# Attention and ReGLU on one core: V's sums of four in three strips on TensorE, and the plan's durations

## The chip, the cores and the metric

The kernel runs on one core of a Trainium2 chip. The time is that of one execution on the device in microseconds; the kernel before takes 375.14 us, the median of three runs (374.98 to 375.96).

The engines are named as in the profile: PE is TensorE's matmul, PEld its weight load, DVE is VectorE, ACT is ScalarE, POOL is GpSimd, SP the engine that issues most DMAs. SPq and POOLq are the queues of SP and POOL as far as they issue or wait.

## The reference

Two kinds of attention are computed for 8 batches of 8 heads, 576 tokens, 64 numbers a head, and added; the result goes through a feed-forward net.

```python
q_d = q.reshape(B, H, Sd, factor, D).mean(axis=3)     # factor 4, Sd 144; the same for k and v
out_d = sm_attn(q_d, k_d, v_d)                        # softmax attention over 144 pooled tokens
out_up = np.repeat(out_d, factor, axis=2)
mask = np.abs(pos[:, None] - pos[None, :]) < factor   # local attention, 3 tokens to either side
...
attn_out = out_up + out_local
x = attn_out.transpose(0, 2, 1, 3).reshape(B * S, H * D)          # 4608 x 512
gate = np.maximum(x @ w_gate, 0.0)                                # 512 -> 1536
return (gate * (x @ w_val)) @ w_out                               # 1536 -> 512
```

## The kernel before

**Pairs.** `pair(p)` (L392) treats two heads of one batch at once; there are 32 pairs, four to a batch. The first four pairs (`hd`) are the head of the kernel. A pair goes through these steps:

- `lq`, `lk` (L419): SP loads q and k of both heads. `cast` (L332, or L331 on ACT) makes them half precision in `c16`.
- T: q and k are transposed. Pairs 0 to 7 (`p < TD`) do it on TensorE (L439) and copy the result out of PSUM (`ev`); later pairs do it by DMA (L470) into `tq`, and one copy, also called `ev`, interleaves it into `qkT`. That copy may run on ACT, POOL or DVE; its planned durations are the tuple `EV` (L50).
- `pl`: sums of four tokens of q and k (L489 on DVE; in the head by extra matmuls, L443).
- S: local scores (L501, 48 matmuls with 32-column weights) and pooled scores (L520, 12 matmuls with 32-column weights that write four strips of 32 partitions). The local softmax follows on DVE, POOL and ACT (`msk` L558, `mx` L561, `sub` L564, `exp` L567, `sm` L584, `rc` L586, `nrm` L588, and `tr`, a transpose in blocks, L594).
- Pooled softmax: `dmx` (L570), `nb` (L573), `exd` (L578, three activations that write the weights into `wd` and their sums into `smd`), `rcd` (L600, the reciprocals), `nrd` (L603, weights times reciprocals).
- W: the pooled weights are transposed, so that the 144 pooled keys stand in two halves of 72 rows. Pairs 0 to 7 do it on TensorE (L612, six transposes) with a copy out of PSUM (`evw`); later pairs by DMA (L626).
- V: `lv` loads v in windows of 32 tokens that overlap (L646, L652), `vc` casts them into `vw16`. For the first 12 pairs (`p < VPOOL`), VP sums four tokens of V on TensorE (L666): `sums_sb` is a matrix of ones and zeros, 128 x 6 x 72, and for each half of the keys six matmuls accumulate into the same 72 rows, one for each block of windows. `vd` copies the sums into `vdz`. Later pairs load v once more (`l4`, L679) and add on POOL (L683, L688).
- The output: L697 (local, 12 matmuls), L705 (pooled, 4 matmuls with `vdz` as weights and the transposed pooled weights as data), `od` (L715), and `xa` (L721), which writes the pair's rows of `xT`.

**Feed-forward.** `first` (L740) makes one block of the hidden layer: matmuls of `xT` with w_gate and with w_val (L755), the rectifier on ACT (L767), the product on DVE (L775). `second` (L787) makes a block of 128 output tokens (L797, three parts of four matmuls), a copy on ACT (L806) and a store (L809).

**PSUM.** Eight banks: 0 to 3 are pool F (feed-forward, and pairs 1 and 2), 4 to 7 pool A (pairs).

**The plan.** No step is issued where the program text has it. Each is an `Op` with an engine (or several, `add_any`), a duration in us, its dependencies, a priority, the banks it needs, and for a DMA a transfer time `xfer`. `list_schedule` (L82) simulates the engines, one DMA channel, the port that DVE and POOL share, the banks and TensorE's instruction fetch with these durations, and each time issues, on the engine that could start first, the ready step of the lowest priority number. An engine that isn't an op's first choice is charged 0.8 us more in the comparison. The order that comes out is fixed: each engine executes its list in that order, waiting at each instruction for what it needs. So a duration in the plan costs no time itself, but it decides the order on all queues. Weight loads have due times that are constants (`W_AT` L42; `WO_T0`, `WO_DT` L43). The loads of a pair from the second batch on are released by `pacers` (L816): the feed-forward block named there must have been computed first.

Of the kernel before, what the change touches and what calls it, by code (L numbers as in the profile page):

```python
# [46 lines left out]
BIAS = 0.8  # L47
STOP = 0.3

EV = (1.4, 1.4, 1.3)  # L50

# [186 lines left out]
def kernel(  # L238
# [36 lines left out]
    def many(n, shape, dt, name):  # L275
        return [pool.tile(shape, dt, name=f"{name}{i}") for i in range(n)]
# [63 lines left out]
    def half(i):  # L340
# [6 lines left out]
                  name="ld_mask")  # L347
    ld_sums = add(SP, 0.2, lambda o: nc.sync.dma_start(sums_sb, sums_dr), prio=5.8, xfer=0.4,
                  name="ld_sums")
# [29 lines left out]
    for g in range(4):  # L379
        for nm, dst, src in (("g", wg_sb, moe_w_gate), ("v", wv_sb, moe_w_val)):  # L380
            w_ld[nm, g] = add(POOL, 0.95, wpiece(dst, src, 384 * g, 384), prio=-40 + g,
                              xfer=2.55, after=W_AT[g], name=f"w{nm}{g}")
# [9 lines left out]
    def pair(p):  # L392
# [25 lines left out]
        def load(src, odd):  # L418
# [4 lines left out]

        lq = add(SP, 0.1, load(q, 0), [free_nat, pace], prio=PQ, xfer=1.1, name=f"lq{p}")
        lk = add(SP, 0.1, load(k, 1), [free_nat, pace], prio=PQ + 0.5, xfer=1.1,
                 name=f"lk{p}")
        casts = ((POOL, 1.55), (DVE, 1.0), (ACT, 1.5)) if hd else (
            (POOL, 1.19), (DVE, 0.9), (ACT, 1.15))
        n2 = 2 * nj
# [120 lines left out]
        if hd:  # L550
            mxo = add(DVE, 0.55, lambda o: nc.vector.tensor_reduce(
                out=mx[S3], in_=lview(), axis=AX.X, op=ALU.max), [Sx, z_w], prio=P + 23,
                name=f"mx{p}")
            sub = add(DVE, 0.62, lambda o: nc.vector.tensor_tensor(
                out=s_, in0=lview(), in1=bc12(mx[S3]), op=ALU.subtract),
                [mxo, b2.get("exp")], prio=P + 24, free=[("S", p)], name=f"sub{p}")
        else:
# [14 lines left out]
            negate=True), [Sd, b3.get("nrd")], prio=P + 22, name=f"dmx{p}")  # L572
        nb = add(POOL, 0.26, lambda o: nc.gpsimd.tensor_scalar(  # L573
            out=nmb[S3][:, 0:3], in0=nmx[S3][:, 0:3], scalar1=scale / 16.0, scalar2=None,
            op0=ALU.mult), [dmax], prio=P + 22.5, name=f"nb{p}")
# [16 lines left out]
        for par in range(2):  # L592
# [7 lines left out]
        rcd = add(DVE, 0.15, lambda o: nc.vector.reciprocal(  # L600
            out=rsd[S3][:, 0:3], in_=smd[S3][:, 0:3]), exd, prio=P + 27.5, name=f"rcd{p}")
        w3 = [[256, 3], [128, 2], [1, 72]]
        r["nrd"] = nrd = add_any(either(lambda o, e: e.tensor_tensor(  # L603
            out=_sap(wd_, 0, 128, 0, w3), in0=_sap(wd_, 0, 128, 0, w3),
            in1=_sap(rsd[S3], 0, 128, 0, [[1, 3], [0, 2], [0, 72]]), op=ALU.mult),
            (POOL, 0.92), (DVE, 0.62)), [rcd], prio=P + 28.5, name=f"nrd{p}", port=(DVE, POOL))

        def emit_W(o):
            for kc in range(2):
                for i in range(3):  # L610
                    n = 3 * kc + i
                    nc.tensor.transpose(half(o.banks[0])[0:72, 128 * n : 128 * n + 128],  # L612
                                        wd_[:, 2 * i + kc, 0:72], ident)
        if p < TD:
            r["W"] = W = add(PE, 0.34, emit_W, [nrd], prio=P + 30, need=(pool_, 1),
                             key=("W", p), name=f"W{p}", n=6)

            evw = add_any(copies(
                _sap(wT[S3], 0, 72, 0, [[48, 6], [2 * SD, 2], [24, 2], [1, 24]]),
                lambda o: _sap(half(W.banks[0]), 0, 72, 0,  # L620
                               [[128, 6], [64, 2], [32, 2], [1, 24]]),
                (ACT, 0.64), (DVE, 0.74)),
                [W, b3.get("V")], prio=P + 31, free=[("W", p)], name=f"evw{p}")
            wcols = lambda hh, kc: _sap(wT[S3], 0, 72, (2 * hh + kc) * SD, [[1, SD]])
        else:
            r["W"] = evw = add(SP, 1.1, lambda o: nc.sync.dma_start(  # L626
                wT[S3], _sap(wd_, 0, 128, 0, [[1, 768]]), transpose=True),
                [nrd, b3.get("V")], prio=P + 30, xfer=0.8, name=f"dW{p}")
            wcols = lambda hh, kc: _sap(wT[S3], 0, 72, 128 * kc + 64 * hh,
                                        [[256, 3], [32, 2], [1, 24]])  # L630
# [6 lines left out]
        for par in range(2):  # L637
# [18 lines left out]
        r["vcast"] = vc = add_any(copies(  # L656
            vw16[S3], lambda o: vw_, (POOL, 1.5), (DVE, 0.97), (ACT, 1.5)),
            lv + behind + [b3.get("V")], prio=P + 26, name=f"vc{p}", port=(DVE, POOL))

        vdz4 = _sap(vdz[S3], 0, 72, 0, [[320, 2], [128, 2], [1, 64]])  # L660
        if p < VPOOL:

            def emit_VP(o):
                for kc in range(2):
                    for i in range(6):
                        nc.tensor.matmul(  # L666
                            out=bank[o.banks[0]][0:72, 128 * kc : 128 * kc + 128],
                            lhsT=sums_sb[:, i, :], rhs=vw16[S3][:, 6 * kc + i, :],
                            start=(i == 0), stop=(i == 5))
            VP = add(PE, 0.8, emit_VP, [vc, ld_sums], prio=P + 27, need=(pool_, 1),  # L670
                     key=("VP", p), name=f"VP{p}", n=12)
            vps = lambda o: _sap(bank[VP.banks[0]], 0, 72, 0, [[64, 2], [128, 2], [1, 64]])
            vdo = add_any(copies(vdz4, vps, (ACT, 0.39), (DVE, 0.41)), [VP, z_vd[S3], b3.get("V")],
                          prio=P + 27.2, free=[("VP", p)], name=f"vd{p}")
        else:
# [19 lines left out]
        def emit_V(o):  # L695
# [178 lines left out]
```

## Time and profile before

| what | us |
|---|---|
| median of three runs | 375.14 |
| the profiled execution | 373.75 |
| its span | 372.0 |
| TensorE busy | 349.3 |
| POOL busy | 211.7 |
| ACT busy | 193.2 |

The chain of work that ended last lies to 65% on PE, to 14% on DMA and to 8% on POOL. The mean granted TensorE clock was 0.995 of full speed.

A row of a group of instructions reads: line, engine, operation, what it writes and reads, partitions x elements and type, count | busy us, mean ns of one | idle time of the engine just before, and who ended it. A row of the timeline reads: start us, duration us, engine, line, what, count, and in square brackets the engine's idle time before it with what released it. Matmuls overlap in a pipeline, so that their own durations overlap too; what a block of them occupies is read from its first start to the start of the next block.

### The profile page before, as it was taken

How to read it: one execution, taken by the hardware profiler on the slowest of the kernel's cores; microseconds unless marked ns; L12 is line 12 of the kernel's file. 1: busy time of each engine (PE TensorE's matmuls, PEld its weight loads, DVE VectorE, ACT ScalarE, POOL GpSimd, SP SyncE). 2: the span in 40 equal slices, each digit the busy share in tenths (PEclk: the TensorE clock that was granted, in tenths of full speed). 3: DMA queues.
4: the chain of work that ended last, by engine and by line, in shares of the span. 5: the costliest groups of instructions: out<-in, count | busy, mean ns of one | idle time of the engine just before them, and what ended most of it. 6: DMA issues, size and time to landing. Idle time of an engine off the chain costs nothing.

```text
span 372.0 us, 11562 instructions
## 1 busy us (share of the span) xinstructions
PE 349.3 (94%) x4728; PEld 194.2 (52%) x4728; DVE 249.2 (67%) x476; ACT 193.2 (52%) x469; POOL 211.7 (57%) x246
## 2 busy tenths in 40 slices
PE   1869999999999999989999998999999999999995
PEld 1657565646655555435555555445545545455442
DVE  3688867657988977867877986877877782222200
ACT  2595747355677554744745564655655543333311
POOL 6698582854868776578778584846785830000000
PEclk9998999999999999999999999999999999999999
DMA  7989999979999699999999989799899820100022
GB/s 189 196 172 234 239 197 244 170 205 217 207 214 201 191 168 234 188 215 204 215 207 212 202 199 215 201 220 193 198 223 221 124 60 28 58 28 31 28 86 85
DMA packets 125271, 64.31 MB, mean 173 GB/s; under 512 B 101026, under 2 KB 112674, under 8 KB 125218
## 3 DMA queue, kind: packets, MB, share of 16 engines
q1 hardware_dynamic: 119394, 58.85, 75.9%
q0 software_dynamic: 5824, 4.72, 8.7%
q8 instruction: 37, 0.61, 0.7%
q14 instruction: 16, 0.13, 0.1%
HBM read 47.03 MB, written 9.44 MB: 152 GB/s over the span
## 4 chain that ended last, share of the span: by engine, by line
PE 65%; DMA 14%; POOL 8%; SPq 4%; issue 4%; DVE 2%; ACT 2%; POOLq 0%; ACTq 0%
PE bank L755 38%; PE bank L797 18%; DMA vw<-in_v_dram 6%; DMA stage<-in_k_dram 5%; PE bank L501 2%; DMA wT<-wd 2%; POOL e L588 2%; DMA wo_sb<-in_moe_w_out_dram 2%; PE bank L697 2%; SPq L419 2%; POOL vw L332 2%; PE bank L705 2%; POOL c L332 1%; SPq L652 1%; PE bank L666 1%
## 5 line engine op out<-in xcount | busy, mean ns | idle before, releaser
L755 PE MATMUL bank<-xT,wg_sb 128*128 128x512 f16 (+1 forms) x768 | 112.8, 286 | 1.4 <-DVE gT L775 1.2
L755 PE MATMUL bank<-xT,wv_sb 128*128 128x512 f16 (+1 forms) x768 | 112.6, 286 | 0.0
L775 DVE TENSOR_TENSOR gT<-r,bank 128x512 f16<-128x512 f16 (+1 forms) x112 | 74.0, 664 | 51.6 <-PE bank L755 48.7
L797 PE MATMUL bank<-wo_sb,gT 128*128 128x512 f16 x432 | 101.0, 379 | 1.0 <-DMA wo_sb<-in_moe_w_out_dram 0.6
L767 ACT ACTIVATE r<-bank 128x512 f16<-128x512 f32 (+1 forms) x112 | 65.0, 583 | 63.0 <-PE bank L755 58.7
L755 PEld LDWEIGHTS <-wg_sb 128*128 128x128 f16 x768 | 49.2, 98 | 44.8 <-issue 2.2
L755 PEld LDWEIGHTS <-wv_sb 128*128 128x128 f16 x768 | 48.8, 98 | 42.0 <-issue 0.2
L797 PEld LDWEIGHTS <-gT 128*128 128x128 f16 x432 | 40.9, 98 | 47.6 <-issue 1.8
L332 POOL CAST c<-stage 128x1152 f16<-128x1152 f32 (+1 forms) x29 | 34.5, 1189 | 25.1 <-DMA stage<-in_k_dram 25.0
L332 POOL CAST vw<-vw 128x1536 f16<-128x1536 f32 x28 | 41.3, 1476 | 11.8 <-DMA vw<-in_v_dram 9.1
L806 ACT COPY y_sb<-bank 128x512 f32<-128x512 f32 x36 | 21.1, 586 | 50.5 <-PE bank L797 49.7
L578 ACT ACTIVATE wd<-bank,nmb 128x144 f16<-128x144 f32 x96 | 35.6, 382 | 18.9 <-POOL nmb L573 18.8
L594 DVE STREAM_TRANSPOSE at<-e 64x384 f16<-64x384 f16 x64 | 36.5, 570 | 11.7 <-POOL e L588 11.0
L489 DVE TENSOR_REDUCE qkd<-qkT 128x288 f16<-128x1152 f16 x28 | 37.5, 1344 | 4.8 <-ACT qkT L331 4.4
L588 POOL TENSOR_TENSOR e<-e,rs 128x384 f16<-128x384 f16 x32 | 26.6, 832 | 15.1 <-DVE rs L586 10.9
L721 DVE TENSOR_TENSOR xT<-bank,od_sb 128x288 f16<-128x288 f32 x64 | 26.4, 451 | 10.9 <-ACT od_sb L715 9.1
L603 POOL TENSOR_TENSOR wd<-wd,rsd 128x432 f16<-128x432 f16 x32 | 28.9, 906 | 3.2 <-DVE rsd L600 2.9
L683 POOL TENSOR_TENSOR vs<-stage 72x512 f32<-72x512 f32 x20 | 25.3, 1267 | 6.5 <-DMA stage<-in_v_dram 6.4
L331 ACT COPY qkT<-tq 128x1152 f16<-128x1152 f16 x21 | 25.3, 1204 | 5.4 <-DMA tq<-c 5.4
L564 POOL TENSOR_TENSOR s_sb<-s_sb,mx 128x384 f32<-128x384 f32 x27 | 22.5, 834 | 6.1 <-DVE mx L561 4.5
L573 POOL TENSOR_SCALAR nmb<-nmx 128x3 f32<-128x3 f32 x32 | 7.4, 232 | 24.8 <-DVE nmx L570 24.8
L584 DVE TENSOR_REDUCE sm<-e 128x12 f32<-128x384 f16 x32 | 17.6, 549 | 5.1 <-ACT e L567 4.9
(57 smaller groups left out, 329.7 us busy)
## 6 DMA issues: line engine op xcount, KB each, us to landing
vw<-in_v_dram SPq DMA_DIRECT2D x126, 96.0 KB, 4.9
stage<-in_q_dram SPq DMA_DIRECT2D x32, 288.0 KB, 5.0
stage<-in_k_dram SPq DMA_DIRECT2D x32, 288.0 KB, 6.9
out_dram<-y_sb SPq DMA_DIRECT2D x36, 256.0 KB, 2.6
stage<-in_v_dram SPq DMA_DIRECT2D x20, 288.0 KB
wg_sb<-in_moe_w_gate_dram POOLq DMA_DIRECT2D x4, 384.0 KB, 8.4
wv_sb<-in_moe_w_val_dram POOLq DMA_DIRECT2D x4, 384.0 KB, 12.1
wo_sb<-in_moe_w_out_dram POOLq DMA_DIRECT2D x4, 384.0 KB, 6.2
```

Of the source, the lines that this page charges most:

```text
L331: return lambda o: nc.scalar.copy(out=dst, in_=src(o))
L332: return lambda o: engine[eng].tensor_copy(out=dst, in_=src(o))
L489: nc.vector.tensor_reduce(out=qkd[S3].rearrange("p (x t) -> p x t", x=2), in_=qk_sums, axis=AX.X, op=ALU.add)
L578: exd.append(add(ACT, 0.37, lambda o, i=i: nc.scalar.activation(out=wd_[:, 2 * i : 2 * i + 2, 0:72], in_=dview()[:, i, :].rearrange("p (k ...
L588: r["nrm"] = nrm = add_any(either(lambda o, e: e.tensor_tensor(out=e_, in0=e_, in1=bc12(rs[S3]), op=ALU.mult), (POOL, 0.84), (DVE, 0.5)), ...
L594: tr.append(add(DVE, 0.575, lambda o, lo=lo: nc.vector.transpose(out=at2[S3][lo : lo + 64, :, lo // 2 : lo // 2 + 32], in_=e_[lo : lo + 64 ...
L603: r["nrd"] = nrd = add_any(either(lambda o, e: e.tensor_tensor(out=_sap(wd_, 0, 128, 0, w3), in0=_sap(wd_, 0, 128, 0, w3), in1=_sap(rsd[S3 ...
L721: nc.vector.tensor_tensor(out=xT[:, kk, t1 % XR : t1 % XR + 288].rearrange("p (t f) -> p t f", f=4), in0=bank[V.banks[hf]][:, 0:288].rearr ...
L755: nc.tensor.matmul(out=bank[(h or o).banks[0]][:, n * x : n * x + n], lhsT=w_sb[:, kk, bass.ts(jj, 128)], rhs=xT[:, kk, t0 % XR : t0 % XR ...
L767: rl = add(ACT, 0.17 + 0.00083 * n * m, lambda o: nc.scalar.activation(out=rt[:, 0 : n * m], in_=bank[f1.banks[0]][:, 0 : n * m], func=AF. ...
L775: gm = add(DVE, 0.15 + 0.00104 * n * m, lambda o: nc.vector.tensor_tensor(out=gT[:, js[0] : js[0] + m, pos : pos + n], in0=rt[:, 0 : n * m ...
L797: nc.tensor.matmul(out=bank[parts[0].banks[0]], lhsT=gT[:, jj, col : col + 128], rhs=wo_sb[:, jj, :], start=(jj == 0), stop=(jj == NJJ - 1))
```

## The change

VP uses six matmuls of 256 columns instead of twelve of 128. `sums_sb` holds only two patterns of 32 columns (24 of them used, 8 zero); the pooled keys of blocks 2g and 2g + 1, 24 in each half, go to strip g, that is to partitions 32g to 32g + 23, and both halves stand side by side in the 256 columns. For these 12 pairs the keys therefore stand in 96 rows, 24 used and 8 unused in each 32: `exd` writes the weights in runs of 24 with a step of 32, `nrd` multiplies in that shape (so `rcd` writes each reciprocal twice), W transposes 96 columns, `evw` and `vd` copy 96 rows, and L705 contracts over 96 rows. The unused places are zeros, which is why `wd` is zeroed whole at the start. Pairs 12 to 31 keep 72 rows.

Besides, planned durations change: the ev copy (ACT and POOL 1.4 to 1.2, DVE 1.3 to 0.68), S (0.80 to 0.67), VP (0.8 to 0.34, 0.4 in the head), casts, subtractions and POOL's small ops by some hundredths, transfers of q and k (1.1 to 1.0 in the head, to 1.3 after it), of the matrix (0.4 to 0.1), and the issue of gate and value weights (0.95 to 0.85).

```diff
+LQ = (1.0, 1.3)
-EV = (1.4, 1.4, 1.3)
+EV = (1.2, 1.2, 0.68)
...
-    sums = np.zeros((128, 6, 72), np.float16)
-    for i in range(6):
+    sums = np.zeros((128, 2, 32), np.float16)
+    for i in range(2):
...
-    vdz = many(3, [72, 2, 2, 128], FP16, "vdz")
+    vdz = many(3, [96, 2, 2, 128], FP16, "vdz")
-    sums_sb = pool.tile([128, 6, 72], FP16, name="sums_sb")
+    sums_sb = pool.tile([128, 256], FP16, name="sums_sb")
-    rsd = many(3, [128, 4], FP32, "rsd")
+    rsd = many(3, [128, 6], FP32, "rsd")
...
-    z_wd = [zeros(wd[s][:, :, 72:128], (POOL, DVE)[s % 2], -88 + s, 0.2) for s in range(3)]
-    z_vd = [zeros(vdz[s][:], POOL, -90 + s, 0.27) for s in range(3)]
+    z_wd = [zeros(wd[s][:], (POOL, DVE)[s % 2], -88 + s, 0.38) for s in range(3)]
+    z_vd = [zeros(vdz[s][:], POOL, -86 + s, 0.3) for s in range(3)]
...
-            r["S"] = Sx = Sd = add(PE, 0.80, emit_S, [*evs, pl], prio=P + 20, need=(pool_, 2),
+            r["S"] = Sx = Sd = add(PE, 0.67, emit_S, [*evs, pl], prio=P + 20, need=(pool_, 2),
...
+        KR = 96 if p < VPOOL else 72
+        kd_cols = [[128, 2], [32, 3], [1, 24]] if p < VPOOL else [[128, 2], [1, 72]]
+        kd_in = [[72, 2], [24, 3], [1, 24]] if p < VPOOL else [[72, 2], [1, 72]]
...
-                out=wd_[:, 2 * i : 2 * i + 2, 0:72],
-                in_=dview()[:, i, :].rearrange("p (k c) -> p k c", k=2), func=AF.Exp,
+                out=_sap(wd_, 0, 128, 256 * i, kd_cols),
+                in_=_sap(dview()[:, i, :], 0, 128, 0, kd_in), func=AF.Exp,
...
-            out=rsd[S3][:, 0:3], in_=smd[S3][:, 0:3]), exd, prio=P + 27.5, name=f"rcd{p}")
-        w3 = [[256, 3], [128, 2], [1, 72]]
+            out=rsd[S3].rearrange("p (i k) -> p i k", k=2),
+            in_=_sap(smd[S3], 0, 128, 0, [[1, 3], [0, 2]])), exd, prio=P + 27.5, name=f"rcd{p}")
+        w3 = [[128, 6], *kd_cols[1:]]
...
-                    nc.tensor.transpose(half(o.banks[0])[0:72, 128 * n : 128 * n + 128],
-                                        wd_[:, 2 * i + kc, 0:72], ident)
+                    nc.tensor.transpose(half(o.banks[0])[0:KR, 128 * n : 128 * n + 128],
+                                        wd_[:, 2 * i + kc, 0:KR], ident)
...
-                for kc in range(2):
-                    for i in range(6):
+                for x in range(2):
+                    for g in range(3):
                         nc.tensor.matmul(
-                            out=bank[o.banks[0]][0:72, 128 * kc : 128 * kc + 128],
-                            lhsT=sums_sb[:, i, :], rhs=vw16[S3][:, 6 * kc + i, :],
-                            start=(i == 0), stop=(i == 5))
-            VP = add(PE, 0.8, emit_VP, [vc, ld_sums], prio=P + 27, need=(pool_, 1),
-                     key=("VP", p), name=f"VP{p}", n=12)
+                            out=bank[o.banks[0]][32 * g : 32 * g + 32, 0:256],
+                            lhsT=sums_sb[:, 32 * x : 32 * x + 32],
+                            rhs=_sap(vw16[S3], 0, 128, 128 * (2 * g + x),
+                                     [[6 * 128, 2], [1, 128]]),
+                            start=(x == 0), stop=(x == 1))
+            VP = add(PE, 0.4 if hd else 0.34, emit_VP, [vc, ld_sums], prio=P + 27, need=(pool_, 1),
+                     key=("VP", p), name=f"VP{p}", n=6)
...
                     nc.tensor.matmul(
-                        out=bank[o.banks[0]][:, 288 : 288 + SD], lhsT=vdz[S3][:, hh, kc, :],
-                        rhs=wcols(hh, kc), start=(n == 0), stop=(n == 3))
+                        out=bank[o.banks[0]][:, 288 : 288 + SD],
+                        lhsT=vdz[S3][0:KR, hh, kc, :],
+                        rhs=wcols(hh, kc), start=(n == 0), stop=(n == 3))
```

More of the change, by code (lines that the diff above doesn't have):

```diff
@@ L422, in load @@
                 _dap(src, base, [[tk * D, nj], [HS, 2], [1, tk * D]]))
[L424 to L428, printed above, removed]
+        lq = add(SP, 0.1, load(q, 0), [free_nat, pace], prio=PQ, xfer=LQ[hd], name=f"lq{p}")
+        lk = add(SP, 0.1, load(k, 1), [free_nat, pace], prio=PQ + 0.5,
+                 xfer=LQ[hd], name=f"lk{p}")
+        casts = ((POOL, 1.47), (DVE, 1.0), (ACT, 1.5)) if hd else (
+            (POOL, 1.15), (DVE, 0.77), (ACT, 1.15))
         n2 = 2 * nj
@@ L618, in pair @@
             evw = add_any(copies(
-                _sap(wT[S3], 0, 72, 0, [[48, 6], [2 * SD, 2], [24, 2], [1, 24]]),
-                lambda o: _sap(half(W.banks[0]), 0, 72, 0,
+                _sap(wT[S3], 0, KR, 0, [[48, 6], [2 * SD, 2], [24, 2], [1, 24]]),
+                lambda o: _sap(half(W.banks[0]), 0, KR, 0,
                                [[128, 6], [64, 2], [32, 2], [1, 24]]),
@@ L656, in pair @@
         r["vcast"] = vc = add_any(copies(
-            vw16[S3], lambda o: vw_, (POOL, 1.5), (DVE, 0.97), (ACT, 1.5)),
+            vw16[S3], lambda o: vw_, (POOL, 1.47), (DVE, 0.97), (ACT, 1.48)),
             lv + behind + [b3.get("V")], prio=P + 26, name=f"vc{p}", port=(DVE, POOL))
-        vdz4 = _sap(vdz[S3], 0, 72, 0, [[320, 2], [128, 2], [1, 64]])
+        vdz4 = _sap(vdz[S3], 0, KR, 0, [[320, 2], [128, 2], [1, 64]])
         if p < VPOOL:
             def emit_VP(o):
-                for kc in range(2):
-                    for i in range(6):
+                for x in range(2):
+                    for g in range(3):
                         nc.tensor.matmul(
-                            out=bank[o.banks[0]][0:72, 128 * kc : 128 * kc + 128],
-                            lhsT=sums_sb[:, i, :], rhs=vw16[S3][:, 6 * kc + i, :],
-                            start=(i == 0), stop=(i == 5))
-            VP = add(PE, 0.8, emit_VP, [vc, ld_sums], prio=P + 27, need=(pool_, 1),
-                     key=("VP", p), name=f"VP{p}", n=12)
-            vps = lambda o: _sap(bank[VP.banks[0]], 0, 72, 0, [[64, 2], [128, 2], [1, 64]])
-            vdo = add_any(copies(vdz4, vps, (ACT, 0.39), (DVE, 0.41)), [VP, z_vd[S3], b3.get("V")],
-                          prio=P + 27.2, free=[("VP", p)], name=f"vd{p}")
+                            out=bank[o.banks[0]][32 * g : 32 * g + 32, 0:256],
[5 more added lines that the diff above has]
+                     key=("VP", p), name=f"VP{p}", n=6)
+            vdo = add_any(copies(
+                vdz4, lambda o: _sap(bank[VP.banks[0]], 0, KR, 0, [[64, 2], [128, 2], [1, 64]]),
+                (ACT, 0.39), (DVE, 0.41)), [VP, z_vd[S3], b3.get("V")], prio=P + 27.2, free=[("VP", p)], name=f"vd{p}")
         else:
```

17 lines of the change are left out of this document (10 added, 7 removed).

## The prediction

> **What bounds the kernel now.** I read the page's totals first, then the busy shares in five stretches of the span.
>
> ```profile
> span 372.0 us, 11562 instructions
> PE 349.3 (94%) x4728; PEld 194.2 (52%) x4728; DVE 249.2 (67%) x476; ACT 193.2 (52%) x469; POOL 211.7 (57%) x246
> ...
> 34.40:75.00 40.60, 40.59 (x604) 23.93 (x602) 31.08 (x58) 22.09 (x59) 25.16 (x30) 1.00 1.18 213
> 75.00:126.00 51.00, 50.38 (x815) 28.20 (x814) 41.19 (x77) 33.81 (x83) 34.38 (x39) 1.00 1.10 207
> 126.00:180.00 54.00, 51.13 (x675) 27.36 (x664) 40.41 (x80) 29.72 (x72) 36.79 (x42) 1.00 1.01 199
> 180.00:270.00 90.00, 88.48 (x1301) 47.82 (x1300) 72.27 (x138) 49.94 (x122) 63.45 (x72) 1.00 0.98 206
> 270.00:300.00 30.00, 29.86 (x401) 15.59 (x400) 22.95 (x44) 16.25 (x41) 20.77 (x24) 1.00 0.93 177
> ```
>
> Columns of the last five rows: the stretch, its length, then busy time of PE, PEld, DVE, ACT and POOL, the granted clock, the DMA share and GB/s. From 34.4 to 300 us TensorE is busy but for 0.01 + 0.62 + 2.87 + 1.52 + 0.14 = 5.2 us, at full clock. After 300 the chain of waits is TensorE's own feed-forward work to the end. So the time is a head of some 34 us, TensorE's work, 5.2 us of stalls, and a short tail. A microsecond of TensorE work removed behind 34.4 is worth a microsecond, unless a stall grows in its place.
>
> The profiled execution took 373.75 us for its span of 372.0. That is 1.4 us under the median of 375.14. I work out differences on the span and subtract them from the median.
>
> **The head** is another matter. These are TensorE's rows there, and the one of DVE that its last wait names:
>
> ```profile
> 20.60 0.44 PE L666 MATMUL bank<-vw,sums_sb 128*72 128x128 f16 x5
> 22.42 1.89 PE L666 MATMUL bank<-vw,sums_sb 128*72 128x128 f16 x31 [1.38 <-issue]
> 26.03 0.53 PE L612 MATMUL bank<-ident_sb,wd 128*72 128x128 f16 x6 [1.71 <-POOL wd L603]
> ...
> 30.06 1.49 PE L666 MATMUL bank<-vw,sums_sb 128*72 128x128 f16 x12
> ...
> 33.68 0.74 PE L439 MATMUL bank<-ident_sb,c 128*128 128x128 f16 x9 [0.69 <-DVE c L332]
> 34.26 0.89 PE L755 MATMUL bank<-xT,wg_sb 128*128 128x512 f16 x3
> ...
> 32.86 0.76 DVE L332 CAST c<-stage 128x1152 f16<-128x1152 f32 x1 [0.82 <-DMA vw<-in_v_dram]
> ```
>
> Four pairs' sums of V (5 + 31 + 12 = 48 matmuls) run here, and behind each block TensorE waits for somebody else: 1.71 us for POOL's weights at 26.03, and at 33.68 for a cast on DVE that had itself waited 0.82 us for a transfer. Shorter sums would lengthen those waits. I count nothing for these four pairs.
>
> **The sums of V** (the VP step). Before, a pair takes twelve matmuls of 128 columns. The price is read from start to start, since ends are modelled:
>
> ```profile
> 81.14 0.83 PE L666 MATMUL bank<-vw,sums_sb 128*72 128x128 f16 x12
> 81.81 1.03 PE L755 MATMUL bank<-xT,wv_sb 128*128 128x512 f16 x4
> 82.67 1.03 PE L755 MATMUL bank<-xT,wg_sb 128*128 128x512 f16 x4
> 83.63 0.52 PE L501 MATMUL bank<-qkT 64*32 64x32 f16 x48
> 83.98 0.38 PE L520 MATMUL bank<-qkd 64*32 64x144 f16 x12
> 84.29 0.60 PE L755 MATMUL bank<-xT,wv_sb 128*128 128x512 f16 x2
> ...
> L666 PE MATMUL bank<-vw,sums_sb x144: 216/219/314, 20.6 to 104.9; 128*72 128x128 f16 x144
> ```
>
> Twelve matmuls hold TensorE from 81.14 to 81.81: 0.67 us. Four of 512 columns take 81.81 to 82.67, so 512 columns cost 0.215 us. After the change a pair has six matmuls of 256 columns into three strips of 32 partitions. The trace has no such matmul. The nearest is L520: 32-column weights, four strips side by side, three rounds of 144 columns. It takes 84.29 - 83.98 = 0.31 us, where 3 x 144 = 432 columns would need 0.181 streamed one behind another; 0.13 lies on top. If three strips overlap as its four do, a pair costs two rounds of 256 columns, 0.215 + 0.13 = 0.345 us, a saving of 0.325. Bounds: with nothing on top 0.215, saving 0.455; with no overlap at all 6 x 256 columns, 0.645 + 0.13 = 0.775, a loss of 0.105. I take 0.325, because L520 uses the same strips; that its rows are 64 and not 128 deep is the doubt.
>
> Of the 144 / 12 = 12 pairs, 48 / 12 = 4 are in the head, so 8 run between 34.4 and 105 us, where TensorE has no slack: 8 x 0.325 = **2.6 us** (bounds 3.6 and -0.8).
>
> **What of it is given back.** The only stall of TensorE in that stretch that names a transfer is this:
>
> ```profile
> 66.77 0.83 PE L666 MATMUL bank<-vw,sums_sb 128*72 128x128 f16 x12
> ...
> 72.75 0.83 PE L666 MATMUL bank<-vw,sums_sb 128*72 128x128 f16 x12
> ...
> 75.62 0.81 PE L797 MATMUL bank<-wo_sb,gT 128*128 128x512 f16 x3 [0.63 <-DMA wo_sb<-in_moe_w_out_dram]
> ```
>
> The second product waits for the last quarter of the output weights, whose due time on POOL is a constant of the plan. The two sums between that issue and the wait (the one at 72.75 and one at 66.77) only make TensorE arrive sooner: up to 2 x 0.325 = 0.65 us returned. The new order may put other work there; I take half, **+0.33**, bounds 0 and 0.65.
>
> **The matrix of the sums** shrinks from 128x6x72 to 128x64 numbers.
>
> ```profile
> sums_sb<-sums SPq DMA_DIRECT2D x1, 108.0 KB, 5.2
> 0.00:10.00 10.00, 2.10 (x24) 1.89 (x24) 3.62 (x9) 2.67 (x4) 7.04 (x15) 1.00 0.75 195
> ```
>
> 108 - 16 = 92 KB at the head's 195 GB/s is 0.47 us less in front of the loads of pairs 2 to 5, and DVE's cast at 33.68 waits for such loads. I take **-0.47**; bound 0, if the cast waits for something else.
>
> **Parts at nothing.** Rows that price them:
>
> ```profile
> L331 ACT COPY wT<-bank 72x576 f16<-72x576 f16 x8 | 5.1, 635 | 1.6 <-PE bank L612 1.6
> L331 ACT COPY qkT<-bank 128x576 f16<-128x576 f16 x8 | 4.8, 655 | 8.0 <-PE bank L439 8.0
> L588 POOL TENSOR_TENSOR e<-e,rs 128x384 f16<-128x384 f16 x32 | 26.6, 832 | 15.1 <-DVE rs L586 10.9 <-ACT r L767 4.0
> L603 POOL TENSOR_TENSOR wd<-wd,rsd 128x432 f16<-128x432 f16 x32 | 28.9, 906 | 3.2 <-DVE rsd L600 2.9 <-PE bank L755 0.2
> 6.10 1.46 POOL L332 CAST c<-stage 96x1536 f16<-96x1536 f32 x1 [0.84 <-DMA stage<-in_k_dram]
> 3.35 0.42 POOL L353 MEMSET at<- 128x384 f32 x1
> 4.58 0.24 POOL L353 MEMSET wd<- 128x168 f32 x1
> 69.17 0.50 PE L612 MATMUL bank<-ident_sb,wd 128*72 128x128 f16 x6
> 69.50 1.99 PE L797 MATMUL bank<-wo_sb,gT 128*128 128x512 f16 x8
> ```
>
> Copies of 576 numbers take the same on 72 and on 128 partitions (635, 655 ns), so 96 rows in the evacuations cost nothing. The normalising product walks in runs of 24 instead of 72: L588 pays 832/384 = 2.17 ns a number in runs of 32, L603 906/432 = 2.10, so at most 0.03 us a pair on POOL, 43% idle. The zeroing of three wd buffers grows from 0.24 to 0.42 us; two on POOL make 0.36 us, inside the 0.84 that POOL waits for its first load (without that wait, 0.36 on the head). The reciprocal of six numbers rather than three stays below L586's twelve. The six transposes of the pooled weights keep their 128 moving columns: 0.33 us from 69.17 to 69.50, 55 ns each.
>
> The Trainium skill speaks against that last point. "TensorE: Matmul & The Clock Gate", section LDWEIGHTS, lets a weight load grow with its columns, about one per 1.2 GHz cycle: 60 ns for 72 columns, 80 for 96. By it, the four pairs behind the head that transpose on TensorE would lose an estimated 4 x 6 x (80 - 55) ns = 0.6 us, and the sum would be 0.6 smaller. The 72-column loads here pass at 55 ns, under the rule's 60, so I leave it out.
>
> **The plan's durations** change no instruction, but they reorder every queue. Pooling's source copy (the ev step) is the largest case:
>
> ```profile
> L331 ACT COPY qkT<-tq 128x1152 f16<-128x1152 f16 x21 | 25.3, 1204 | 5.4 <-DMA tq<-c 5.4
> L332 DVE COPY qkT<-tq 128x1152 f16<-128x1152 f16 x2 | 1.4, 676 | 1.2 <-DMA tq<-c 1.2
> ```
>
> With 0.68 for DVE and the planner's penalty of 0.8 for an engine that isn't named first, DVE gets the copy once ACT would be free 0.28 us later than DVE; before it was 0.70. So some of the 21 move: 1.20 us off ACT, 0.68 onto DVE each. Both engines have idle time, 48% and 33%. The score step S, planned at 0.80, is now 0.67, which is what 83.63 to 84.29 shows. What the new order does to the 5.2 us of stalls has no row. Its bounds are all of them gone and as much again, -5.2 to +5.2; I take 0, because the stalls' causes (late loads, late POOL work) stay.
>
> **Sum:** -2.6 + 0.33 - 0.47 = -2.75 us, so 375.14 - 2.75 = **372.4 us**.
>
> **Rivals.**
>
> *The order gets better too.* The 2.87 us of stalls from 126 to 180 come from TensorE standing at a place in its fixed order where a partner is late:
>
> ```profile
> 167.40 0.86 PE L755 MATMUL bank<-xT,wg_sb 128*128 128x64 f16 x24 [1.18 <-DVE gT L775]
> ...
> 177.26 0.46 PE L697 MATMUL bank<-at,vw 128*128 128x48 f16 x12 [0.76 <-DVE at L594]
> ```
>
> True durations, load times among them, could put other work there. All of it gone as well: 369.5. Against it: the partners' lateness comes from transfers (the DMA share is 1.01 there), which no entry for an engine makes punctual.
>
> *Absorbed.* All eight sums lie before 105 us. If the pairs from 126 on come when loads and POOL allow, and not when TensorE does, TensorE only reaches its stalls 2.3 us (2.6 - 0.33) sooner and waits there. What is left is 0.47: 374.7. For it, the DMA share of 1.01; against it, those loads are issued by pacers that are tied to TensorE's own units and move forward with them.
>
> *The strips don't run side by side.* Then 8 x 0.105 is lost, less 0.47: 375.5. L520 is against it, its half depth for it.
>
> *DVE becomes the gate* (slower). The product gT on DVE frees the banks that TensorE's next units need. DVE is 81% busy from 75 to 126 us (41.19 of 51), TensorE has waited 1.18 us for it at 167.40, and this row shows what moved work can cost:
>
> ```profile
> L564 DVE TENSOR_TENSOR s_sb<-s_sb,mx 128x384 f32<-128x384 f32 x1 | 1.1, 1097 | 0.0
> ```
>
> Every ev copy that lands on DVE just ahead of a product holds it back 0.68 us. From 2.75 / 0.68 = 4 such copies on, the gain is gone; eight of them cost 5.4 and give 377.8. The one subtraction that DVE took over from POOL lasted 1097 ns, where the plan says 560. The Trainium skill, "SBUF — State Buffer", has DVE and GpSimd take an exclusive lock on a shared port pair, the later one blocked for the whole instruction; the 1097 ns agree with it. Against this rival: DVE idles a third of the time, and the planner counts what it moves.
>
> **How the numbers follow.** Chances: forecast 0.55, better order 0.12, absorbed 0.11, strips in series 0.05, DVE the gate 0.17. The forecast's own range is 370.0 to 373.9, from the sums' bounds with the give-back. The range reaches down to the better order (369.5, a little below) and up through absorbed and series into the lower part of the DVE case: 368.8 to 377.0. A measurement tells 0.3% from nothing, 1.1 us: under 374.0 is faster, over 376.3 slower. Faster: 0.53 of the forecast, 0.12 of the better order and 0.02 of absorbed, 0.67. Within: 0.02 + 0.09 + 0.04 = 0.15. Slower: 0.17 + 0.01 = 0.18.
>
> **What would show it.** In the changed profile a pair's six sum matmuls in mid-kernel should take about 0.345 us from their first start to the next operation's; near 0.775 means series. The transposes at 96 columns should stay at 0.33. TensorE's idle time from 34.4 to 300 should be near 5.5 us: under 3 speaks for the better order, over 8 for absorbed (stalls ended by loads or POOL) or for DVE (ended by gT). The DVE copies out of tq should number more than 2. The first feed-forward matmul should start near 33.8. I am wrong if the sums keep their 0.67 or if stalls take up more than 2.7 us.

## The result and the profile after

The changed kernel is slower by 0.9%. It takes 378.56 us (median of 18 runs) beside 375.93 for the kernel before on the same chips: ratio 1.0087, 95% interval 1.0062 to 1.0112. Ratios, here and below, are worked out from the fast executions alone, since some executions of either kernel are over 1.5% above its fastest, so they are not the quotients of these medians. Forecast were 372.4 us, and a range of 368.8 to 377.0 that doesn't hold the time. Single executions of either kernel differ by 4 us and more, so ratios of many runs decide here, and profiles show where.

The page's first lines, and the same five stretches as in the prediction (stretch, length, busy PE, PEld, DVE, ACT, POOL, clock, DMA share, GB/s), of the changed kernel:

```profile
span 377.4 us, 11426 instructions
PE 348.4 (92%) x4656; PEld 188.9 (50%) x4656; DVE 248.7 (66%) x475; ACT 190.2 (50%) x467; POOL 215.7 (57%) x249
...
34.40:75.00 40.60, 36.71 (x556) 20.13 (x554) 29.57 (x56) 24.63 (x60) 21.19 (x28) 1.00 1.06 187
75.00:126.00 51.00, 51.00 (x752) 26.33 (x749) 39.28 (x75) 31.52 (x74) 34.23 (x38) 1.00 1.06 211
126.00:180.00 54.00, 49.40 (x728) 27.53 (x727) 40.65 (x78) 27.57 (x70) 38.29 (x45) 1.00 1.03 196
180.00:270.00 90.00, 85.64 (x1191) 45.41 (x1190) 70.06 (x135) 49.70 (x128) 67.00 (x75) 1.00 0.97 206
270.00:300.00 30.00, 29.90 (x432) 16.19 (x431) 24.75 (x48) 14.69 (x40) 23.40 (x25) 1.00 1.08 202
```

TensorE's idle time from 34.4 to 300 us is 3.89 + 0 + 4.60 + 4.36 + 0.10 = 12.95 us; before it was 5.2. That is 7.8 us of new waiting in this execution. The strips themselves do what the prediction said. From the timeline of TensorE in the changed kernel:

```profile
81.92 1.03 PE L765 MATMUL bank<-xT,wg_sb 128*128 128x512 f16 x4
82.88 0.40 PE L673 MATMUL bank<-vw,sums_sb 128*32 128x256 f16 x6
83.21 1.04 PE L765 MATMUL bank<-xT,wv_sb 128*128 128x512 f16 x4
84.08 1.03 PE L765 MATMUL bank<-xT,wg_sb 128*128 128x512 f16 x4
```

From 82.88 to 83.21 are 0.33 us (forecast 0.345). But the four matmuls before it take 82.88 - 81.92 = 0.96 us, and the four after it 84.08 - 83.21 = 0.87. So 0.09 us lies ahead of the first strip; the prediction read the price of the strips from their own first start and missed it.

Where TensorE waits, and for whom (from 34.4 us on: us in total, times, longest): first the changed kernel, then the kernel before.

```profile
PE bank L714 <- DMA wT<-wd: 5.2, 4, 1.9
PE bank L706 <- DVE at L600: 2.0, 3, 1.1
PE bank L522 <- ACT wd L584: 1.8, 2, 1.0
PE bank L765 <- DMA wv_sb<-in_moe_w_val_dram: 1.6, 2, 1.2
PE bank L619 <- POOL wd L610: 1.4, 1, 1.4
PE bank L807 <- issue: 0.9, 1, 0.9
```

```profile
PE bank L755 <- DVE gT L775: 1.2, 1, 1.2
PE bank L697 <- POOL vs L683: 1.1, 1, 1.1
...
PE bank L705 <- DMA wT<-wd: 0.2, 1, 0.2
```

The new place is the pooled output (L714, in the kernel before L705), which waits 5.2 us for pooled weights that a DMA transposes; the score step (L522) waits for ScalarE too. "issue" names no cause: it is idle time in which the profile shows nothing that TensorE waited for. Two places in the timeline of TensorE, changed kernel:

```profile
68.08 1.68 PE L807 MATMUL bank<-wo_sb,gT 128*128 128x512 f16 x7
70.67 0.38 PE L807 MATMUL bank<-wo_sb,gT 128*128 128x512 f16 x1 [0.90 <-issue]
70.97 0.40 PE L673 MATMUL bank<-vw,sums_sb 128*32 128x256 f16 x6
72.76 0.54 PE L619 MATMUL bank<-ident_sb,wd 128*96 128x128 f16 x6 [1.39 <-POOL wd L610]
...
204.72 0.41 PE L714 MATMUL bank<-wT,vdz 72*128 72x144 f16 x4 [1.88 <-DMA wT<-wd]
```

The first hole, 0.90 + 1.39 = 2.3 us, ends when POOL has multiplied a pair's weights (L610); the second ends with a transfer. What POOL did before that product:

```profile
70.15 0.83 POOL L566 TENSOR_TENSOR s_sb<-s_sb,mx 128x384 f32<-128x384 f32 x1 [0.15 <-DVE mx L563]
70.92 0.84 POOL L377 DMA_DIRECT2D wo_sb<-in_moe_w_out_dram  x1
71.79 0.92 POOL L610 TENSOR_TENSOR wd<-wd,rsd 128x432 f16<-128x432 f16 x1
```

The reciprocals that L610 needs were there at 70.16, but in POOL's list a subtraction and the issue of a load of output weights stand ahead of it, so that it begins 1.6 us later. In the kernel before, POOL multiplies at 67.70 and issues that load after it, at 68.76.

### The profile page after: what moved, and what is told of

Same layout as the page of the kernel before. It is cut to its first block, busy times and chain, and to the rows that moved or that the text cites. A ratio compares the mean times of both kernels' runs of the same rounds, so it can differ in the third digit from the quotient of the medians.

```text
span 377.4 us, 11426 instructions
## 1 busy us (share of the span) xinstructions
PE 348.4 (92%) x4656; PEld 188.9 (50%) x4656; DVE 248.7 (66%) x475; ACT 190.2 (50%) x467; POOL 215.7 (57%) x249
## 4 chain that ended last, share of the span: by engine, by line
PE 53%; DMA 19%; POOL 10%; issue 5%; SPq 5%; DVE 4%; ACT 2%; POOLq 0%; DVEq 0%; ACTq 0%
PE bank L765 32%; PE bank L807 16%; DMA wv_sb<-in_moe_w_val_dram 5%; DMA stage<-in_k_dram 5%; DMA stage<-in_v_dram 3%; SPq L421 2%; POOL c L333 2%; DMA tq<-c 2%; POOL vs L692 2%; POOL e L594 2%; DMA wT<-wd 1%; PE bank L706 1%; PE bank L503 1%; DMA vw<-in_v_dram 1%; PE bank L714 1%
## 5 line engine op out<-in xcount | busy, mean ns | idle before, releaser
L333 POOL CAST c<-stage 128x1152 f16<-128x1152 f32 (+1 forms) x31 | 36.7, 1188 | 25.6 <-DMA stage<-in_k_dram 22.4
L333 POOL CAST vw<-vw 128x1536 f16<-128x1536 f32 x29 | 42.5, 1465 | 2.9 <-DMA vw<-in_v_dram 2.5
L594 POOL TENSOR_TENSOR e<-e,rs 128x384 f16<-128x384 f16 x31 | 25.8, 832 | 16.2 <-DVE rs L592 10.5
L610 POOL TENSOR_TENSOR wd<-wd,rsd 128x432 f16<-128x432 f16 x32 | 29.8, 933 | 8.2 <-DVE rsd L606 7.5
L566 POOL TENSOR_TENSOR s_sb<-s_sb,mx 128x384 f32<-128x384 f32 x28 | 23.3, 832 | 7.6 <-DVE mx L563 7.6
L584 ACT ACTIVATION_READ_ACCUMULATOR wd<-bank,nmb 128x1 f32 x96 | 19.7, 205 | 0.0
```

The lines of the kernel that those rows point to most:

```text
L333: return lambda o: engine[eng].tensor_copy(out=dst, in_=src(o))
L594: r["nrm"] = nrm = add_any(either(lambda o, e: e.tensor_tensor(out=e_, in0=e_, in1=bc12(rs[S3]), op=ALU.mult), (POOL, 0.84), (DVE, 0.5)), ...
```

## The experiments

Theories, as they stood: A, the new order costs; B, the new shapes cost; C, late transfers set the pace and swallow what TensorE saves; D, the order has waits of its own that no transfer explains. Ratios are to the kernel before on the same chip, with 95% intervals.

**The two halves of the change, each alone.** The first kernel has the strips, and every duration given to the planner is the old one, so that each engine's list of steps is that of the kernel before. The second has the old sums in exactly the order of the changed kernel.

```diff
 # strips, old order: the changed kernel with
-LQ = (1.0, 1.3)
+LQ = (1.1, 1.1)
-EV = (1.2, 1.2, 0.68)
+EV = (1.4, 1.4, 1.3)
...
 # old sums, new order: the kernel before with
-EV = (1.4, 1.4, 1.3)
+EV = (1.2, 1.2, 0.68)
...
```

> The changed instructions (strips, 96 rows, small matrix) in exactly the order of the kernel before: every duration given to the planner is the old one, so each engine's list of steps is the same as before. Theory A, the order is what costs: TensorE's work falls by 8 x 0.34 us and little new waiting comes, so 2 to 3 us faster than before (ratio 0.992 to 0.995), stalls from 34.4 to 300 us of 5 to 6 us. Theory B, the new shapes themselves slow the pairs (weights in runs of 24, 96-row transposes): not faster than before, ratio 1.00 to 1.01, with stalls like the changed kernel's 13 us. Theory C, transfers and not TensorE set the pace, so that a shorter TensorE only waits more: ratio 0.998 to 1.002, stalls of 7.5 to 8 us.

> The instructions of before in exactly the order of the changed kernel: only the planner's durations are the new ones. Theory A, the order costs: 0.87% of the change plus the sums' 2.7 us that it doesn't have, ratio to before 1.010 to 1.017. Theory B, the shapes cost: back at before, ratio 0.998 to 1.003. Theory C: as slow as the changed kernel and no slower, ratio 1.007 to 1.010, since 2.7 us of TensorE work more only fill its waits.

Strips in the old order: 0.9978 (0.994 to 1.0017). Old sums in the new order: 1.0088 (1.0048 to 1.0129), as slow as the full change, which is C's answer (A had 1.010 to 1.017). So the order carries the loss, and B falls. In the new order nothing of the strips' saving shows in the time. In the old one it is 0.8 us by the ratio, and the interval reaches from 2.3 us saved to 0.6 lost, so this run does not settle how much arrives there. In the profile of the first, stalls rose from 5.2 to 6.8 us; in this stretch TensorE idled 2.7 us, before 0.6:

```profile
75.00:126.00 51.00, 48.26 (x732) 24.84 (x731) 40.61 (x74) 32.04 (x76) 35.08 (x40) 1.00 1.02 197
...
125.80 0.41 PE L714 MATMUL bank<-wT,vdz 96*128 96x144 f16 x4 [1.84 <-DMA wT<-wd]
```

**One planned value put back.**

```diff
-LQ = (1.0, 1.3)
+LQ = (1.1, 1.1)
 # the other kernel:
-            r["S"] = Sx = Sd = add(PE, 0.67, emit_S, [*evs, pl], prio=P + 20, need=(pool_, 2),
+            r["S"] = Sx = Sd = add(PE, 0.80, emit_S, [*evs, pl], prio=P + 20, need=(pool_, 2),
```

> The changed kernel with one planned value put back: the transfers of q and k count 1.1 us again (instead of 1.3 in the head, 1.0 after it). Theory A1, the plan believes in loads that come too early, and TensorE then stands before them: the stalls from 126 to 270 us fall from 9 to under 5, ratio to before 0.99 to 1.00. Theory A2, the loads' value isn't it: ratio stays at 1.005 to 1.012.

> The changed kernel with one planned value put back: the score step S counts 0.80 us on TensorE again instead of 0.67. Theory A3, the old value was slack in the plan (0.13 us in each of 28 pairs) which the chip's late transfers and POOL work used up: stalls from 126 to 270 us fall from 9 to under 6, ratio 0.99 to 1.00. Theory A2 of the other kernel (loads) or no single value: ratio 1.005 to 1.012.

Loads: 1.0063 (1.0016 to 1.0111). Score step: 1.0057 (1.0016 to 1.0099). Neither value alone is the cause. With the old score step the stalls from 126 to 270 us did fall in its profile, from 9.0 to 4.8 us, as A3 had it, but 4.3 us stand from 34 to 75, and the time stayed. Later both TensorE values went back together, `VP` at 0.8 and S at 0.80:

> The changed kernel with the planned durations of TensorE's two steps put back together: S 0.80 and VP 0.80 with twelve matmuls. Theory A3, those two were the slack that covered late transfers: ratio to before 0.990 to 0.999, near the strips in the old order (0.998). Rival, no single pair of values, the order's margins before the transposed weights decide: ratio 1.004 to 1.012.

1.0181 (1.0101 to 1.0261), slower still and above both answers. So the old values were not useful slack.

**Fewer bytes, same orders.** In pairs 4 to 30 three of twelve blocks of v are loaded, and of V's second load two of 72 rows; these kernels leave out the part of the output that the rest of V gives.

```diff
-                    i0, i1 = 0, 12
+                    i0, i1 = 0, 12 if p < 4 or p == NP - 1 else 3
-                v4_.rearrange("p (h c) e -> p h c e", h=2),
-                _dap(v, base, [[4 * D, 72], [HS, 2], [72 * 4 * D, 2], [1, 4 * D]])),
+                v4_[0:2].rearrange("p (h c) e -> p h c e", h=2),
+                _dap(v, base, [[4 * D, 2], [HS, 2], [72 * 4 * D, 2], [1, 4 * D]])),
```

> The changed kernel, same order, with fewer bytes to load: from pair 4 on the windows of v load 3 of 12 blocks, and the extra load of v for the sums of pairs 12 to 31 takes 2 of 72 rows (the rest of V is stale, so the part of the output that V gives is left out). 31 x 0.29 MB x 0.75 and 20 x 0.28 MB less, about 13 of 64 MB. Theory C, late transfers are what TensorE waits for: the stalls from 34.4 to 300 us fall from 13 to under 4, ratio to before 0.970 to 0.978. Theory D, the waits are the order's own (POOL, DVE and ACT in the wrong turn): stalls stay above 9, ratio 0.995 to 1.010.

> The kernel before with the same loads cut in the same way and its own order. Theory C: stalls from 5 to under 3, and with both kernels relieved the changed one is the faster by its smaller TensorE work and earlier start, 2 to 4 us less than this one. Theory D: ratio 0.995 to 1.000, and the changed kernel stays 2 to 4 us slower than this one.

> The strips in the old order (the first experiment) with the loads cut in the same way. Theory C, the 2.7 us of TensorE were real and went into waits for transfers: 2 to 3 us less than the kernel before with cut loads. Rival, other steps wait for something that cut loads don't help (POOL): within 1 us of it.

Changed kernel 369.37 us, 0.9817 (0.976 to 0.9874); kernel before 367.0, 0.9757 (0.9705 to 0.981); strips in the old order 366.18, 0.9739 (0.9677 to 0.9802). Busy rows from 126 to 270 us, changed kernel first, then the kernel before:

```profile
126.00:180.00 54.00, 53.38 (x780) 29.85 (x781) 44.29 (x87) 30.47 (x77) 42.47 (x47) 1.00 0.75 155
180.00:270.00 90.00, 90.00 (x1239) 48.02 (x1236) 73.52 (x141) 50.32 (x130) 69.12 (x77) 1.00 0.69 155
```

```profile
126.00:180.00 54.00, 54.00 (x788) 30.09 (x780) 44.49 (x85) 32.51 (x76) 40.40 (x46) 1.00 0.76 157
180.00:270.00 90.00, 90.00 (x1227) 47.92 (x1226) 74.08 (x141) 51.67 (x130) 65.44 (x76) 1.00 0.69 152
```

With the DMA share at 0.7 instead of 1.0, TensorE is busy without a gap in nearly all of it. C holds for these stretches, in both orders. From 34.4 to 300 us the stalls fell to 3.5 us in the changed kernel and to 0.6 in the kernel before, as C had it. But the changed kernel's 0.9817 falls short of C's 0.970 to 0.978 (its interval reaches into it), and it stays 2.4 us behind the kernel before, which C had the other way round. Its remaining hole is its own:

```profile
67.97 0.40 PE L673 MATMUL bank<-vw,sums_sb 128*32 128x256 f16 x6
70.83 0.54 PE L619 MATMUL bank<-ident_sb,wd 128*96 128x128 f16 x6 [2.46 <-POOL wd L610]
```

That is the first hole from above, and POOL again issues the output weights (68.98) before it multiplies (69.85). So D holds for one place. Here the strips' own worth can be read best: old order, cut loads, first the old sums, then the strips.

```profile
50.89 1.03 PE L755 MATMUL bank<-xT,wv_sb 128*128 128x512 f16 x4
51.76 0.83 PE L666 MATMUL bank<-vw,sums_sb 128*72 128x128 f16 x12
52.43 0.86 PE L755 MATMUL bank<-xT,wg_sb 128*128 128x64 f16 x24
```

```profile
52.04 1.03 PE L765 MATMUL bank<-xT,wv_sb 128*128 128x512 f16 x4
53.00 0.40 PE L673 MATMUL bank<-vw,sums_sb 128*32 128x256 f16 x6
53.33 0.87 PE L765 MATMUL bank<-xT,wg_sb 128*128 128x64 f16 x24
```

The four matmuls ahead of the sums take 51.76 - 50.89 = 0.87 us in the one and 53.00 - 52.04 = 0.96 in the other. A pair saves 0.67 - 0.33 - 0.09 = 0.25 us, eight pairs 2.0. Measured were 0.8 between the medians; waits of 0.9 us from 34.4 us on (0.45 at 40.06 without a cause in the profile, 0.44 at 42.82 for value weights), against one of 0.6 for output weights with the old sums, are part of the difference; the rest is not accounted for. So C's 2 to 3 us did not come, its rival's answer (within 1 us) did.

**An order that expects transfers later.** From the start of its issue, the plan lets the transfer that transposes pooled weights land after 1.1 + 0.8 + 2.0 = 3.9 us at the earliest: issue, transfer and the constant `DMA_LAT`. In the traces the median is 4.5 us for the kernel before, 4.8 for the changed one and 5.3 for the old sums in its order; with the cut loads it is 3.6 for the kernel before. So with all loads the median lies 0.6 to 1.4 us behind that earliest time, and with cut loads it does not. One constant of the planner, nothing else:

```diff
-DMA_T0, DMA_LAT = 0.9, 2.0
+DMA_T0, DMA_LAT = 0.9, 3.0
```

> The changed kernel with one constant of the planner raised: a transfer lands 3.0 us after its slot on the modelled channel, not 2.0, so that the order puts its users later. Theory C with the plan as remedy: the waits for transposed weights and loads shrink, stalls from 13 to under 8, ratio to before 0.99 to 1.00. If the lateness is not a constant but a shortage, or the order is simply another draw: ratio 1.003 to 1.012.

> The kernel before, its order planned with transfers that land 3.0 us after their slot instead of 2.0. Theory C1, every order of this planner gains when it allows for late transfers: ratio to before 0.985 to 0.995, stalls under 5. Theory C2, the new durations need the allowance and the old ones carried it already (TensorE steps planned too long): ratio 0.998 to 1.010.

> The changed kernel planned with transfers 4.0 us after their slot. If the allowance is the cause of the gain at 3.0 (0.989), more of it keeps most of the gain, ratio 0.985 to 0.997, the waits for transposed weights (5.2 us in the changed kernel, 1.4 at 3.0) under 1.5. If the gain at 3.0 was one lucky order: ratio 1.00 to 1.012 and waits of 3 us or more.

> The order of the changed kernel planned at 3.0 us, with the old sums of twelve matmuls of 128 columns in 72 rows. With TensorE near its bound there, the strips' worth shows: 8 x 0.245 = 2.0 us more than the strips in the same order (strips: 0.33 us and 0.09 for entering them, against 0.67), ratio to before 0.992 to 0.997. If waits swallow the strips' gain in a good order too: within 0.8 us of the strips, ratio 0.987 to 0.991.

Changed kernel at 3.0: 371.56 us, 0.9886 (0.9817 to 0.9955). Kernel before at 3.0: 370.47, 0.9868 (0.9805 to 0.993). Changed kernel at 4.0: 369.40, 0.9843 (0.9783 to 0.9903). The waits of the last one, from 34.4 us on:

```profile
PE bank L714 <- DMA wT<-wd: 1.1, 2, 0.6
PE bank L619 <- POOL wd L610: 1.0, 2, 0.8
PE bank L673 <- DVE sm L590: 1.0, 1, 1.0
PE bank L765 <- DVE xT L731: 0.8, 1, 0.8
```

No single wait is over 1.0 us, and L714 waits 1.1 in place of 5.2. The kernel before gains as well, so that C1 holds: the allowance helps whether the durations are the old or the new ones. The old sums in the new order at 3.0 gave 373.3 us, 0.9943 (0.9894 to 0.9991), beside 0.9886 for the strips in the same order: a difference of 2.1 us (0.0057 x 376), what eight times 0.25 make, though the two intervals overlap.

**Is an order without that allowance a draw?** Two kernels of before, each with a small correction (the first for all casts, the second for one step of POOL), and the allowance for the transposed weights alone.

```diff
-        casts = ((POOL, 1.55), (DVE, 1.0), (ACT, 1.5)) if hd else (
-            (POOL, 1.19), (DVE, 0.9), (ACT, 1.15))
+        casts = ((POOL, 1.47), (DVE, 1.0), (ACT, 1.5)) if hd else (
+            (POOL, 1.15), (DVE, 0.77), (ACT, 1.15))
...
-            vw16[S3], lambda o: vw_, (POOL, 1.5), (DVE, 0.97), (ACT, 1.5)),
+            vw16[S3], lambda o: vw_, (POOL, 1.47), (DVE, 0.97), (ACT, 1.48)),
 # the second kernel:
-        nb = add(POOL, 0.26, lambda o: nc.gpsimd.tensor_scalar(
+        nb = add(POOL, 0.23, lambda o: nc.gpsimd.tensor_scalar(
 # the third, from the changed kernel:
-                o.end = dma_free + DMA_LAT
+                o.end = dma_free + DMA_LAT + (2.0 if o.name.startswith("dW") else 0.0)
```

> The kernel before, with only the planned durations of the casts corrected by hundredths (POOL 1.55 to 1.47 and 1.19 to 1.15, DVE 0.9 to 0.77, POOL 1.50 to 1.47 and ACT 1.50 to 1.48 for v). No instruction changes; the order does. If an order without allowance is a draw: off by 0.4% or more either way, ratio under 0.996 or over 1.004. If a correction this small does little and the loss needs the large ones: ratio 0.997 to 1.003.

> The kernel before, with only the planned duration of POOL's smallest step (nb) changed from 0.26 to 0.23. The same two answers: a draw, ratio under 0.996 or over 1.004; or nothing, 0.997 to 1.003.

> The changed kernel, planned with transfers at 2.0 us again, but the transposed pooled weights (dW) at 4.0. If the wait before L714 is what the allowance removes: that wait falls from 5.2 us to under 1.5 and most of the gain comes, ratio to before 0.984 to 0.995. If the loads' lateness matters as much: the wait falls too, but others grow, ratio 0.997 to 1.010.

Casts: 1.0078 (1.0032 to 1.0125), nearly the whole loss of the change from corrections of 0.02 to 0.13 us in the plan; on that chip single executions of the kernel before lie between 370.9 and 382.3 us, so that the size is rough. The smallest step: 1.0016 (0.9976 to 1.0055), nothing. The transposed weights alone: 1.0122 (1.0068 to 1.0176). There L714 is gone from the list of waits, but others came:

```profile
PE bank L706 <- DVE at L600: 3.8, 2, 2.7
PE bank L522 <- DVE qkd L491: 2.5, 2, 2.2
PE bank L619 <- POOL wd L610: 2.5, 1, 2.5
```

So the waits before L714 are one place where the lateness shows, not the only one. The last two kernels take the durations of two slow orders and change only the constant, to 4.0:

> The slowest order of the study (the changed kernel with S and VP planned at 0.80, ratio 1.018), planned with transfers 4.0 us after their slot instead of 2.0. If the allowance is the cause: ratio to before 0.980 to 0.994, waits for transposed weights under 1.5 us. If the good orders were good draws: 0.997 to 1.020, anywhere in the spread seen without it.

> The kernel before with corrected casts (ratio 1.008), planned with transfers 4.0 us after their slot. If the allowance is the cause: ratio 0.982 to 0.996 even with the old sums. If draws: 0.997 to 1.015.

0.9896 (0.9866 to 0.9926) for the order that had 1.0181, and 0.9858 (0.9818 to 0.9899) for the one that had 1.0078. In the first, L714 still waited 2.3 us in its profile, over the 1.5 expected, yet the time came. The seven new orders planned at 2.0 (one of them with later transposed weights) lie between 1.0016 and 1.0181, and the six kernels at 3.0 or 4.0 between 0.9843 and 0.9943. Each of the four sets of durations that were planned both ways gained. So the allowance is the cause of the gain, and not a lucky order. None of the seven orders planned at 2.0 is clearly faster than the kernel before, and six are clearly slower; its own order was a good one among such orders, and nothing here says how it was found. The strips at 4.0 have the lowest ratio of the kernels that load everything (0.9843), but the old sums with corrected casts at 4.0 (0.9858) cannot be told from it.

## Why the prediction was wrong

The section on the change has one thing the wrong way round. It says that transfers of q and k are planned at 1.0 in the head and 1.3 after it. `LQ[hd]` takes the second value where `hd` is true, so 1.3 holds in the head and 1.0 after it: the new plan trusts the steady loads more than the old one did, 1.1. Putting 1.1 back did not mend it (1.0063).

Point by point:

- **The sums, -2.6 us.** The mechanism was right: three strips of full depth run side by side, 0.33 us forecast at 0.345. The size was off by the 0.09 us ahead of them: 2.0 us, not 2.6. The rows quoted in the prediction held it: 82.67 to 83.63 are 0.96 us for four matmuls of 512 columns ahead of the score step, against 0.86 for the four before. The Trainium skill has the rule, "TensorEngine Tiling (Array Packing)", Key Properties: changing the tiling mode drains TensorE; the 0.09 us agree.
- **The matrix of the sums, -0.47 us on the head.** Nothing of it came. Strips in the old order have their first feed-forward matmul at 34.30 us, the kernel before at 34.26; it still stands behind the same wait for a cast on DVE. The 33.17 of the changed kernel (33.8 was forecast) belongs to the new order, which has 33.21 with the old sums.

```profile
33.63 0.83 PE L441 MATMUL bank<-ident_sb,c 128*128 128x128 f16 x9 [0.82 <-DVE c L333]
34.30 0.81 PE L765 MATMUL bank<-xT,wg_sb 128*128 128x512 f16 x3
```

- **Given back, +0.33 us** at the wait for output weights. That wait is gone in the changed kernel, but there TensorE waits 1.6 us for the value weights.
- **The plan's durations, 0.** This is the step that failed. The prediction bounded it by -5.2 and +5.2 and took the middle "because the stalls' causes (late loads, late POOL work) stay". They stay, but their size depends on the order, and they are not quite these: before, the waits name DVE for 2.4 us, POOL for 1.1 and transfers for only 0.8; in the changed kernel they name transfers for 5.2 + 1.6 = 6.8. The order alone, with the old sums, costs 0.88% of the time, about 3.3 us, where the sum has 0; in its one profile it idles TensorE 8.6 us, 3.4 more than before. The rise of 7.8 us in the changed kernel is outside the bound of 5.2, but it is not the order's alone: the strips shorten TensorE's work, and in this order that became waiting. So the -2.6 us does not show in the time either. The range, built round 0 with a slow case of 0.17, ended short of the result.
- **"DVE becomes the gate"**, the only clearly slower rival, is not what happened. The ev copies did not move; the groups of the changed kernel have as many on each engine as before. TensorE's waits for DVE (2.0 us before L706) are one entry among six. Nor does the row of 1097 ns show the lock by itself: POOL was issuing a load from 68.76 to 69.60 us, and its next cast, begun at 69.61 while that subtraction still ran, took 1.76 us where such casts take 1.48 on average.

```profile
L332 ACT COPY qkT<-tq 128x1152 f16<-128x1152 f16 x21 | 25.2, 1199 | 6.4 <-DMA tq<-c 6.4
L333 DVE COPY qkT<-tq 128x1152 f16<-128x1152 f16 x2 | 1.5, 754 | 0.0
L610 POOL TENSOR_TENSOR wd<-wd,rsd 128x432 f16<-128x432 f16 x32 | 29.8, 933 | 8.2 <-DVE rsd L606 7.5 <-DMA vw<-in_v_dram 0.3
```

- **"Absorbed"** was the nearest rival: its sign, stalls over 8 us that loads or POOL end, is nearly what the profile has, with 6.8 us for transfers (5.2 of them transposes) and 1.4 for POOL. Strips in the old order came out at 0.9978 where it had 374.7 / 375.14 = 0.9988, though that interval holds a full saving too. It was given 0.11, and it has no loss by the order.
- **The forecast's own range**, 370.0 to 373.9, does not follow from its bounds. They give 375.14 - 3.64 - 0.47 = 371.0 at best and 375.14 + 0.84 + 0.65 = 376.6 at worst; neither holds the result.
- The parts at nothing stayed small: the normalising product (L610) took 933 ns on average instead of 906, and six transposes of 96 columns again took 0.35 us or so:

```profile
52.48 0.52 PE L619 MATMUL bank<-ident_sb,wd 128*96 128x128 f16 x6
52.83 0.51 PE L765 MATMUL bank<-xT,wv_sb 128*128 128x64 f16 x12
```

What stays open: which single durations made the changed order what it is, why transfers land later than planned (the queue, the small packets or the issue on SP were not told apart), which transfers the allowance has to cover, whether 4.0 us is better than 3.0, since the intervals overlap, and how much of the strips' 2.0 us a good order turns into time: no pair of kernels shows it clear of noise.

## What to carry to other kernels

Where a program fixes the order of every engine ahead of time, a change of planned durations is a new order, and its cost can't be taken as zero even where the change is small; test the layout in the old order and the order with the old layout. Before durations are made exact, the plan needs an allowance for what it can't know: here one constant for late transfers gave times 0.6 to 1.6% below the kernel before, and 1.3% or more below the same durations planned without it (the ratios differ by 0.013 to 0.029), more than the 2.0 us of the strips. Read the price of a matmul block from the start of the last matmul ahead of it, not from its own first start.

## What the runs showed of the hardware

Two things had not been expected. Entering a block of 32-column strips lengthened the last 512-column matmul ahead of it by 0.09 us, for the sums as for the scores: from its start to the next are 0.31 us at each such place after 35 us in both kernels, and 0.22 ahead of the old sums with their 72 columns. And the granted clock in the head was lower: from 20 to 30 us it was 0.90 before and 0.64 in the changed kernel (the third number from the right; the kernel before first).

```profile
20.00:30.00 10.00, 6.60 (x128) 6.06 (x117) 8.13 (x20) 8.62 (x27) 9.89 (x13) 0.90 0.96 195
```

```profile
20.00:30.00 10.00, 7.23 (x139) 5.25 (x124) 8.56 (x20) 8.04 (x27) 9.43 (x13) 0.64 0.91 197
```

Over all traces it is 0.61 to 0.83 there with the strips and 0.83 to 1.00 with the old sums. That the strips leave TensorE less work in the head may be the reason; no run tests it. The feed-forward part began as early as with the old sums in the same order (33.21), whose clock was 0.93, so that the lower clock cost nothing that shows:

```profile
33.17 0.81 PE L765 MATMUL bank<-xT,wg_sb 128*128 128x512 f16 x3
```
